# Setup in the MLP's buffers, layer 2's weights decoded beside layer 1, half of the first stores issued by ScalarE: one core of a Trainium2

## The chip, the cores and the metric

One core of one Trainium2 chip runs the whole program. The metric is the device time of one execution in microseconds (us); each kernel is run several times and its median is used. TensorE (PE in the rows) multiplies, VectorE (DVE) and ScalarE (ACT) do element-wise work and empty PSUM, GpSimd (POOL) does element-wise work on SBUF, and SyncE's queue (SP) issues the DMAs. PEld is TensorE's loading of weights.

## The reference

```python
def _attn_ref(x, w_r, w_i, b_r, b_i):          # x: 8 x 3136 x 256
    X = np.fft.rfft(x, axis=1)
    Yr = Xr @ w_r - Xi @ w_i + b_r
    Yi = Xr @ w_i + Xi @ w_r + b_i
    lam = 0.01
    Yr = np.sign(Yr) * np.maximum(np.abs(Yr) - lam, 0.0)
    Yi = np.sign(Yi) * np.maximum(np.abs(Yi) - lam, 0.0)
    y = np.fft.irfft(Y, n=x.shape[1], axis=1)

def _moe_ref(x, U, V, w_ch1, w_ch2):           # U: 3136 x 32, V: 32 x 3136
    xt = x.transpose(0, 2, 1)
    h = xt @ U @ V
    u = x + h.transpose(0, 2, 1)
    ch = np.maximum(u @ w_ch1, 0.0) @ w_ch2    # 256 -> 1024 -> 256
    return u + ch
```

U, V, w_ch1 and w_ch2 arrive as 64-bit floats, and the kernel makes 32-bit numbers of their words itself; this is what "decode" means below.

## The kernel before, in words

**The work.** The Fourier transform over 3136 = 49 x 64 positions is a chain of stages for each of the 8 batches. Stage A multiplies by the 49-point matrix (`a_mm`, PSUM tiles `psa`, 16 units of 98x512 for a batch) and stores the result in DRAM (`gd`, through the tiles `gs`). Stage B reads it back (`t`), multiplies by the 64-point matrix and its twiddles (`fb`, PSUM `psb`). The mix multiplies by the complex weights (PSUM `psy` in batch 0; `psq` and `pst` later), then comes the shrinking (`rl`, `ys`). Stage C goes back over 64 points (`psc`) and stores in DRAM (`zd`, through `zs`). Stage D reads that (`zt`) and multiplies by constants and by U at once (PSUM `psd`, 32 steps a batch); the result lies in SBUF as `xq`, and its product with U is summed in `pa`, turned by two transposes (`psp`) into `pt`. The MLP then goes over 6 windows of 512 positions a batch: `u_prep` adds the product with V (`psv`) to `xq` and splits it into a high and a low part (`oa`, `ob`, `oc`, `od`), layer 1 takes seven products of blocks with the prepared weights `w1t` (PSUM `psx`, `psy`, `psz`), its ReLU gives `rh` and `rl`, layer 2 multiplies by `w2h` and `w2l` (PSUM `pso`), and the sum goes out through `os`. Most products are three matmuls of split operands; A's first units and stages B and D multiply unsplit 32-bit operands.

**What lies beside what.** While the MLP of batch b runs, A of batch b + 2 and B to D of batch b + 1 are put between its chunks. Batch 0 has nothing to lie beside: its stages A to D run alone, with the decoding of the weights between them. Half of A of batch 1 is done early: units 0 to 3 while D of batch 0 waits for its first input, units 4 to 7 behind D (`turn`).

**The decoding.** `load_words` brings 512 (for V 392) 64-bit words a partition, `decode` makes 32-bit numbers of them with two ScalarE and six or seven VectorE instructions on tiles of 128x512 (`dm`, `dlf`, `dq`, `dp`). There are two pieces of V, two of U, four of `w_ch2` (into `w2h`, `w2l`) and four of `w_ch1` (into `wa`), in the order of the list `jobs`; `combine` makes the seven blocks of `w1t` out of the four `wa`.

**What sets the order.** The code records all operations with their tiles, and a list scheduler (`order`, `forward`, `backward`) with a cost for each operation gives each engine one fixed order, which the hardware then follows. Before the change the recording has two phases. Phase 0 is batch 0 up to `turn`, phase 1 is the MLP with all that lies beside it, and `forward` lets no operation of phase 1 stand ahead of one of phase 0 on its engine. The two phases have pools of SBUF tiles of their own, `setup` (named `sp` in the code) and `mp`, which take the same memory one after the other: `mp` is opened when `setup` is closed.

```python
    for phase, p in enumerate((sp, mp)):
        with tc.tile_pool(name=p.name, bufs=p.bufs) as p.real, tc.manual_schedule():
            prog.trace(engines, phase)
```

**Constants of D.** In batch 0 D's right-hand side is one tile `du` (98 x 32 x 130: 98 numbers of the constant and 32 of the product with U). For later batches a `dt` tile takes the constant's part from the input and the other 32 from a copy in DRAM (`dud`), two DMAs for each four steps.

Of the kernel before, what the change touches and what calls it, by code (L numbers as in the profile page):

```python
# [143 lines left out]
class _Op:  # L144
    __slots__ = "n eng name args kw out cost lag start preds succs unit at phase".split()


class _Program:


    def __init__(self):
        self.ops, self.phase = [], 0
# [10 lines left out]
    def record(self, eng, name, args, kw):  # L163
        op = _Op()
        op.n, op.eng, op.name, op.args, op.kw, op.phase = len(self.ops), eng, name, args, kw, self.phase
        op.preds, op.succs = {}, []
        out = kw["out"] if "out" in kw else args[0]
        views = [v for v in list(args) + list(kw.values()) if isinstance(v, _View)]
        op.out = out
        self.cost(op, out, [v for v in views if v is not out])  # L170
        for v in views:
            self.access(op, v, v is out)
        self.ops.append(op)
        return op

    def cost(self, op, out, ins):
        n = out.ids.size // out.shape[0] if isinstance(out, _View) else 1
        sb = not any(v.buf.space == "psum" for v in ins)
        if op.eng == "pe":
# [16 lines left out]
        else:  # L196
            some = out if isinstance(out, _View) else ins[0]

            op.cost, op.lag = max(0.6, some.ids.size / 53760), 2.2
# [32 lines left out]
    def order(self):  # L232
# [24 lines left out]
        def gap(e, op):  # L257

            if e.eng == op.eng and e.eng != "sp":
# [10 lines left out]
        frees = {}  # L270
        for bufs in tags.values():
            k = max(b.bufs for b in bufs)
            for a, b in zip(bufs, bufs[k:]):
                for op in a.users:
                    frees.setdefault(op.n, []).append(b.first[0])

        after, ahead = [{} for _ in units], [{} for _ in units]
        for k, u in enumerate(units):
            for op in u:
                for s in op.succs + frees.get(op.n, []):  # L280
# [3 lines left out]
        for k, d in enumerate(after):  # L284
            for j, g in d.items():
                ahead[j][k] = g
# [11 lines left out]
        for _ in range(PASSES):  # L298
            end, starts = self.forward(units, size, tags, gap, late)
            if best is None or end < best[0]:  # L300
                best = end, starts, self.idle
            late = self.backward(units, size, after, ahead, starts, end)
# [6 lines left out]
    def backward(self, units, size, after, ahead, starts, end):  # L309

        free = {}
# [37 lines left out]
    def forward(self, units, size, tags, gap, late):  # L349
# [3 lines left out]
        left = {(e, p): 0 for e in engines for p in range(self.phase + 2)}  # L353
        wait = [0] * len(units)
        avail = [0.0] * len(units)
        for k, u in enumerate(units):
            left[u[0].eng, u[0].phase] += 1
            for op in u:
                wait[k] += sum(e.unit != k for e in op.preds.values())
        closed = {}  # L360
        for k, u in enumerate(units):
            if u[0].phase and any(left[u[0].eng, p] for p in range(u[0].phase)):
                wait[k] += 1
                closed.setdefault((u[0].eng, u[0].phase), []).append(k)
        slots = {key: [0.0] * max(b.bufs for b in bufs) for key, bufs in tags.items()}
# [17 lines left out]
        def grant(key):  # L383
            bufs = tags[key]
            while turn[key] < len(bufs) and slots[key]:
                b = bufs[turn[key]]
                turn[key] += 1
                t = _heapq.heappop(slots[key])
# [11 lines left out]
        while done < len(units):  # L400
# [20 lines left out]
            for op in units[k]:  # L421
# [8 lines left out]
                for b in bs.values():  # L430
                    b.left -= 1
                    b.end = max(b.end, op.start + op.cost + op.lag)
                    if b.left == 0:
                        _heapq.heappush(slots[b.key], b.end)
                        grant(b.key)
            p = units[k][0].phase
            left[e, p] -= 1
            if left[e, p] == 0:
                for q in range(p + 1, self.phase + 1):
                    if not any(left[e, r] for r in range(q)):  # L440
                        for j in closed.pop((e, q), []):
                            release(j, free[e])
        return max(free.values()), starts

    def trace(self, engines, phase):
# [3 lines left out]
        for op in sorted((o for o in self.ops if o.phase == phase), key=lambda o: (o.start, o.n)):  # L449
# [5 lines left out]
def fft_mix_moe_kernel(  # L455
# [24 lines left out]
    fp, qp, sp, mp = _Pool("fp", 2), _Pool("qp", 2), _Pool("setup", 1), _Pool("mp", 1)  # L480
# [49 lines left out]
    dud = dram.tile([NP, NI, R], F32, name="dud")  # L530
# [37 lines left out]
    def a_mm(b, u):  # L568
# [12 lines left out]
        dma.dma_start(gv[:, 2 * u : 2 * u + 2, :], gs)  # L581
# [29 lines left out]
    def load_fb(b, q):  # L611
# [3 lines left out]
        if b:  # L615
            fbt = fp.tile([128, 2, 128], F32, tag="fb", name=f"fb_{b}_{q}")
        else:
            fbt = first_w["pool"].tile([128, 2, 128], F32, tag="fb0", name=f"fb_{b}_{q}", bufs=5)
# [269 lines left out]
    def d_load(b, t, du):  # L888
        z_load(b, 2 * t)
        z_load(b, 2 * t + 1)  # L890
        if du is None:
            dt_ = mp.tile([NP, TI, NP + R], F32, tag="dt", name=f"dt_{b}_{t}", bufs=2)
            i = slice(TI * t, TI * t + TI)
            dma.dma_start(dt_[:, :, 0:NP], c_fd[:, i, 0:NP])
            dma.dma_start(dt_[:, :, NP:], dud[:, i, :])
        else:
            dt_ = du[:, TI * t : TI * t + TI, :]
# [61 lines left out]
    words = {}  # L959

    def load_words(src, shape, name):
# [7 lines left out]
    def decode(name, hi=None, lo=None, full=None):  # L969
# [43 lines left out]
    first_w["pool"] = sp  # L1013
# [4 lines left out]
    wz = sp.tile([128, 256], F32, name="wz")  # L1018
# [28 lines left out]
    b4r = sp.tile([128, D], F32R, name="b4r")  # L1047
    one = sp.tile([128, 128], F32R, name="one")
# [26 lines left out]
    fcs = sp.tile([128, 192], F32, name="fcs")  # L1075
# [16 lines left out]
    us = sp.tile([NP, NI, R], F32, name="us")  # L1092
    vt = dict(r=sp.tile([128, 64], F32, name="vraw"))
# [6 lines left out]
    du = sp.tile([NP, NI, NP + R], F32, name="du")  # L1100
# [17 lines left out]
    def make_ud(c):  # L1118
        ps = psm([128, 512], f"psu_{c}")
        for k in range(8):  # L1120
            mm = pe.matmul(
# [585 lines left out]
```

## Time and profile before

| | |
|---|---|
| median of 3 runs | 1751.05 us (1749.66 to 1752.8) |
| the profiled execution | 1750.79 us, its span from the first to the last instruction 1749.0 us |
| TensorE busy | 1685.0 us, 96% of the span |
| VectorE busy | 1330.8 us, 76% |
| ScalarE busy | 1029.7 us, 59% |
| GpSimd busy | 579.1 us, 33% |
| DMA queue of SP | 203.38 MB, 45.1% of the 16 DMA engines' span |
| mean granted clock of TensorE | 0.978 of full speed (2.4 GHz) |

The first instruction starts at 0. Stage A of batch 0 runs to about 27 us, B to C from 34 to 101 us, D from 108.8 to 126.3 us. Layer 1 starts at 174.09 us. Matmuls are pipelined, so a row's own duration is longer than its step: 12 matmuls of 128x256 stand in the chain of waits with 1.44 us. The granted clock shows whether TensorE ran at 1.2 (0.5) or 2.4 GHz (1.0).

### The profile page before, as it was taken

What the parts mean: (1) busy time and instruction counts of PE and PEld (TensorE: products, weight loads), DVE (VectorE), ACT (ScalarE), POOL (GpSimd) and SP (SyncE); (2) the same over time, 40 slices, a digit from 0 to 9 for tenths busy, and PEclk for the clock granted to TensorE, in tenths of its full rate; (3) what the DMA queues carried; (4) which work ended last, traced back from release to release, by engine and by line L of the source; (5) the groups of instructions that cost most, each with busy time, mean ns of one, the idle gap of its engine ahead of it and who ended that gap; (6) DMA issues with size and microseconds to landing.
All of it is one profiled execution on the core that took longest, in us unless ns stands there. A gap on an engine that the chain in (4) does not pass through costs nothing.

```text
span 1749.0 us, 31800 instructions
## 1 busy us (share of the span) xinstructions
PE 1685.0 (96%) x11071; PEld 1512.7 (86%) x11071; DVE 1330.8 (76%) x2476; ACT 1029.7 (59%) x2206; POOL 579.1 (33%) x508
## 2 busy tenths in 40 slices
PE   7982999999999999999999999999999999999998
PEld 4971788999898898999988889999989998998997
DVE  2647799788767887699866988689876887757774
ACT  2763677566667665555557665556566565554443
POOL 0211464233434543133343543223344232212221
PEclk8985999999999999999999999999999999999999
DMA  6865465543466543523357543443356432332112
GB/s 214 215 199 138 131 175 147 144 107 84 105 169 179 157 111 91 126 75 87 78 147 202 155 129 78 113 101 88 79 128 184 110 83 37 80 97 51 37 31 37
DMA packets 284690, 205.42 MB, mean 117 GB/s; under 512 B 173506, under 2 KB 237766, under 8 KB 284530
## 3 DMA queue, kind: packets, MB, share of 16 engines
q1 hardware_dynamic: 284530, 203.38, 45.1%
q8 instruction: 89, 1.46, 0.3%
q14 instruction: 71, 0.58, 0.1%
HBM read 124.11 MB, written 79.18 MB: 116 GB/s over the span
## 4 chain that ended last, share of the span: by engine, by line
PE 90%; DVE 5%; DMA 2%; issue 1%; ACT 0%; POOL 0%; SPq 0%; DVEq 0%; POOLq 0%; ACTq 0%
PE pso L451 30%; PE psy L451 17%; PE psx L451 8%; PE psd L451 7%; PE psq L451 7%; PE psb L451 5%; PE psa L451 4%; PE psz L451 4%; PE psc L451 4%; PE pst L451 3%; DVE ys L451 1%; PE psv L451 1%; DVE rl L451 1%; DMA xt<-in_x_dram 1%; DVE tb L451 0%
## 5 line engine op out<-in xcount | busy, mean ns | idle before, releaser
L451 PE MATMUL pso<-rh,w2h 128*128 128x512 f32 x784 | 251.0, 402 | 0.0
L451 PE MATMUL pso<-rl,w2h 128*128 128x512 f32 x784 | 244.1, 393 | 1.0 <-DVE rl L451 1.0
L451 PE MATMUL pso<-rh,w2l 128*128 128x512 f32 x784 | 244.3, 393 | 0.0
L451 POOL TENSOR_TENSOR xl<-xt,xh 98x512 fp32r<-98x512 f32 x104 | 139.4, 1340 | 241.3 <-ACT xh L451 241.0
L451 DVE SCALAR_TENSOR_TENSOR ys<-tb,rl 64x256 f32<-64x256 f32 x350 | 195.2, 558 | 10.6 <-ACT rl L451 5.9
L451 POOL TENSOR_TENSOR yl<-ys,yh 128x512 fp32r<-128x512 f32 (+1 forms) x101 | 133.9, 1326 | 197.4 <-ACT yh L451 194.5
L451 ACT ACTIVATE rh<-s 128x512 fp32r<-128x512 f32 x196 | 123.4, 631 | 97.1 <-DVE s L451 95.6
L451 PEld LDWEIGHTS pso<-rl,w2h 128*128 128x128 f32 x784 | 147.2, 188 | 34.8 <-DVE rl L451 1.8
L451 PEld LDWEIGHTS pso<-rh,w2l 128*128 128x128 f32 x784 | 147.6, 188 | 33.9
L451 DVE SCALAR_TENSOR_TENSOR rl<-s,rh 128x512 fp32r<-128x512 f32 x196 | 159.9, 819 | 9.3 <-ACT rh L451 6.7
L451 POOL TENSOR_TENSOR tl<-ts,th 128x256 fp32r<-128x256 f32 x88 | 70.3, 799 | 235.3 <-ACT th L451 188.8
L451 PEld LDWEIGHTS pso<-rh,w2h 128*128 128x128 f32 x784 | 126.0, 189 | 6.9
L451 PE MATMUL psy<-odh,w1t 128*128 128x256 f32 x784 | 125.5, 282 | 0.7 <-DVE s L451 0.7
L451 PE MATMUL psd<-dt,zt 98*128 98x130 f32 x896 | 124.6, 275 | 0.1
L451 ACT ACTIVATE xq<-psd 128x196 f32<-128x196 f32 x256 | 84.0, 332 | 69.0 <-PE psd L451 60.5
L451 DVE TENSOR_TENSOR v<-v,psy 128x512 f32<-128x512 f32 x98 | 67.0, 684 | 75.4 <-ACT v L451 36.0
L451 PEld LDWEIGHTS psd<-dt,zt 98*128 98x128 f32 x896 | 117.3, 190 | 6.0 <-DVE tt L451 0.3
L451 PEld LDWEIGHTS psy<-odh,w1t 128*128 128x128 f32 x784 | 110.4, 188 | 7.9 <-DVE s L451 1.5
L451 PE MATMUL psb<-fb,t 128*128 128x128 f32 (+1 forms) x800 | 107.0, 277 | 8.4 <-DVE tb L451 6.6
L451 POOL TENSOR_TENSOR ocl<-xq,och 128x256 fp32r<-128x256 f32 x47 | 35.6, 758 | 235.3 <-ACT och L451 235.2
L451 PEld LDWEIGHTS psb<-fb,t 128*128 128x128 f32 (+1 forms) x800 | 100.2, 193 | 13.6 <-DVE tb L451 7.5
L451 ACT ACTIVATE xsh<-psb 128x256 fp32r<-128x256 f32 (+1 forms) x176 | 58.0, 379 | 80.2 <-PE psb L451 80.1
(208 smaller groups left out, 4551.6 us busy)
## 6 DMA issues: line engine op xcount, KB each, us to landing
gd<-gs SPq DMA_DIRECT2D x128, 196.0 KB
zt<-zd SPq DMA_DIRECT2D x128, 196.0 KB
t<-gd SPq DMA_DIRECT2D x192, 128.0 KB
zd<-zs SPq DMA_DIRECT2D x192, 128.0 KB
out_dram<-os SPq DMA_DIRECT2D x192, 128.0 KB
xt<-in_x_dram SPq DMA_DIRECT2D x112, 196.0 KB
fb<-in_fb_dram SPq DMA_DIRECT2D x96, 128.0 KB
vw<-vd SPq DMA_DIRECT2D x96, 128.0 KB
```

Source lines behind the costliest of these rows:

```text
L451: call(*[real(a) for a in op.args], **{k: real(a) for k, a in op.kw.items()})
```

## The change

- **No border.** The pool `setup`, the phases and their gate in `forward` are gone. Every tile of the setup takes a tag of the MLP's pool `mp` (or of `fp`): the loaded words `dw` lie in `rh`, the decoder's tiles in `sv`, U and `wa` in `rl`, `du` as eight tiles of four steps in `oh`, `ol` and `dt`.
- **Layer 2's weights.** The four `w_ch2` pieces leave `jobs`. `w2_unit` decodes them after the setup: piece 0 ahead of window 0, the others as side work at 1, 5 and 9 of window 0's 16 chunks. They are loaded into `ww` (a third slot of `xq`) and `rh`.
- **The order of the rest.** `jobs` is now V, U, the first piece of `w_ch1`, V's second step, the other three pieces, `combine`.
- **Stores of A.** In batch 0 the stores of the even units are issued by ScalarE's queue.
- **Constants of D.** `dud` holds whole rows of 130; eight stores write them from `du`, and a `dt` tile is one DMA of 98x520 numbers.
- **The scheduler** takes a DMA's size as size/67500, at least 0.55, and `backward` follows the slots that `forward` really gave.

```diff
-    fp, qp, sp, mp = _Pool("fp", 2), _Pool("qp", 2), _Pool("setup", 1), _Pool("mp", 1)
+    fp, qp, mp = _Pool("fp", 2), _Pool("qp", 2), _Pool("mp", 1)
...
-        dma.dma_start(gv[:, 2 * u : 2 * u + 2, :], gs)
+        (dma if b or u % 2 else act).dma_start(gv[:, 2 * u : 2 * u + 2, :], gs)
...
-            dma.dma_start(dt_[:, :, 0:NP], c_fd[:, i, 0:NP])
-            dma.dma_start(dt_[:, :, NP:], dud[:, i, :])
+            dma.dma_start(dt_, dud[:, i, :])
...
-        w = first_w["pool"].tile([128, 1024], U32, tag="dw", name="dw_%s%d%d" % name, bufs=3)
+        if name in place:
+            w = place[name]
+        else:
+            w = mp.tile([128, 1024], U32, tag="rh", name="dw_%s%d%d" % name, bufs=3)
...
-    du = sp.tile([NP, NI, NP + R], F32, name="du")
+    du = [
+        mp.tile([NP, TI, NP + R], F32, tag=tg, name=f"du_{t}", bufs=2 if tg == "dt" else 3)
+        for t, tg in enumerate(("oh", "ol", "oh", "ol", "oh", "ol", "dt", "dt"))
+    ]
...
-    jw2 = [(lambda f=f: load_w(2, f), lambda f=f: decode_w2(f)) for f in range(4)]
-    jobs += jw2[:1]
-    jobs += [(load_v4, make_v), (lambda: None, lambda: iter(()))]
-    jobs += jw2[1:]
     jobs += [
         (lambda i=i, h=h: load_w(1, i, h), lambda i=i, h=h: decode_w1(i, h))
         for h in range(2)
         for i in range(2)
     ]
+    jobs[5:5] = [(load_v4, make_v)]
...
-    on(133, lambda: dma.dma_start(dud, du[:, :, NP:]))
+    for t in range(NT):
+        on(116 + 2 * t, lambda t=t: dma.dma_start(dud[:, TI * t : TI * t + TI, :], du[t]))
...
-    prog.phase = 1
...
+    ww = qp.tile([128, 3, 1024], U32, tag="xq", name="ww", bufs=3)
+
+    def w2_unit(n):
+        f = (0, 2, 1, 3)[n]
+        if n < 3:
+            place[2, f, 0] = ww[:, n]
+        load_w(2, f)
+        for _ in decode_w2(f):
+            pass
+
+    w2_unit(0)
...
+                    side += [(at, lambda n=n: w2_unit(n + 1)) for n, at in enumerate((1, 5, 9))]
...
-    for phase, p in enumerate((sp, mp)):
-        with tc.tile_pool(name=p.name, bufs=p.bufs) as p.real, tc.manual_schedule():
-            prog.trace(engines, phase)
+    with tc.manual_schedule():
+        prog.trace(engines)
```

Three places of the fixed orders follow. The first is VectorE from the end of D of batch 0: `pa` is the running sum over D's steps, `pr` and `pt` prepare it for the product with V. Before:

```order
L451 TENSOR_TENSOR pa_1166<-pa_1166,psd_31_1338 128x64
L451 COPY pr_1348<-pa_1166 128x256
L451 TENSOR_SCALAR dm_1353<-dm_1353 128x512
L451 TENSOR_TENSOR pt_1357<-psp_1351,pt_1357 64x256
L451 TENSOR_SCALAR dm_1353<-dm_1353 128x512
L451 SCALAR_TENSOR_TENSOR dq_1368<-dw_1024,dm_1353 128x512
L451 TENSOR_SCALAR dp_210_1371<-dq_1368 128x512
L451 TENSOR_TENSOR dp_210_1371<-dlf_1361,dp_210_1371 128x512
L451 TENSOR_TENSOR dq_1368<-dq_1368,w2h 128x512
L451 TENSOR_TENSOR w2l<-dq_1368,dp_210_1371 128x512
```

Now, from the last instruction of `combine` on:

```order
L442 TENSOR_TENSOR w1t<-s_1277,w1t 128x512
L442 TENSOR_TENSOR pa_1250<-pa_1250,psd_26_1409 128x64
L442 TENSOR_TENSOR pa_1250<-pa_1250,psd_27_1415 128x64
L442 TENSOR_TENSOR pa_1250<-pa_1250,psd_28_1421 128x64
L442 TENSOR_TENSOR pa_1250<-pa_1250,psd_29_1426 128x64
L442 TENSOR_TENSOR pa_1250<-pa_1250,psd_30_1431 128x64
L442 TENSOR_TENSOR pa_1250<-pa_1250,psd_31_1439 128x64
L442 COPY pr_1452<-pa_1250 128x256
L442 TENSOR_SCALAR dm_1454<-dm_1454 128x512 x2
L442 TENSOR_TENSOR pt_1462<-psp_1456,pt_1462 64x256
L442 SCALAR_TENSOR_TENSOR dm_1454<-ww,dm_1454 128x512
L442 TENSOR_TENSOR xq_0_1238<-xq_0_1238,psv_0_1472 128x16x32
```

Before, three pieces of `w_ch2`, four of `w_ch1` and `combine` stood between `pt` and the first sum with `psv`; now all of `w_ch1` stands ahead of D's end, and only three instructions of the first piece of `w_ch2` stand there.

The second place is TensorE from there to the first product of layer 1 (`psy<-obh,w1t`). Before, behind `psd_31`, `psp` and units 4 and 5 of A (`psa`, batch 1):

```order
L451 MATMUL psa_6_1522<-xt_6_1411,fas 98x512
L451 MATMUL psv_0_1537<-vw_1526,pt_1357 128x512
L451 MATMUL psv_1_1539<-vw_1526,pt_1357 128x512
L451 MATMUL psa_7_1557<-xt_7_1461,fas 98x512
L451 MATMUL psa_8_1565<-xh_8_1551,fah 98x512
L451 MATMUL psa_8_1565<-xh_8_1551,fal 98x512
L451 MATMUL psa_8_1565<-xl_8_1555,fah 98x512
L451 MATMUL psr_1575<-vr,pt_1357 128x64 x2
L451 MATMUL psa_9_1589<-xh_9_1571,fah 98x512
L451 MATMUL psa_9_1589<-xh_9_1571,fal 98x512
L451 MATMUL psa_9_1589<-xl_9_1580,fah 98x512
L451 MATMUL psy_0_1599<-obh_1577,w1t 128x256 x4
```

Now:

```order
L442 MATMUL psd_31_1439<-du_1177,zt_15_1391 128x130 x2
L442 MATMUL psa_4_1444<-xt_4_1282,fas 98x512
L442 MATMUL psp_1456<-ident,pr_1452 128x128 x2
L442 MATMUL psv_0_1472<-vw_1240,pt_1462 128x512
L442 MATMUL psv_1_1476<-vw_1240,pt_1462 128x512
L442 MATMUL psa_5_1478<-xt_5_1450,fas 98x512
L442 MATMUL psa_6_1493<-xt_6_1468,fas 98x512
L442 MATMUL psa_7_1502<-xt_7_1474,fas 98x512
L442 MATMUL psy_0_1512<-obh_1491,w1t 128x256 x4
L442 MATMUL psy_0_1512<-obl_1499,w1t 128x256 x2
```

Units 8 and 9 of A and `psr` have moved behind the first products of layer 1.

The third place is SP's queue behind D's last input `zt_15`. Before, some `vd` stores on (`dw` are words to decode, `xt` the inputs of A's units 4 to 8):

```order
L451 DMA dw_1366<-in_moe_w_ch_dram 128x2x512
L451 DMA dw_1373<-in_moe_w_ch_dram 128x2x512
L451 DMA dw_1380<-in_moe_w_ch_dram 128x1024
L451 DMA xt_4_1388<-in_x_dram 98x512
L451 DMA dw_1393<-in_moe_w_ch_dram 128x1024
L451 DMA xt_5_1404<-in_x_dram 98x512
L451 DMA gd_1117<-gs_3_1148 98x512
L451 DMA xt_6_1411<-in_x_dram 98x512
```

Now:

```order
L442 DMA zt_15_1391<-zd_599 98x512
L442 DMA ww<-in_moe_w_ch_dram 128x2x512
L442 DMA dud<-du_852 98x520
L442 DMA gd_1203<-gs_2_1226 98x512
L442 DMA vw_1240<-vd 64x512
L442 DMA xt_5_1450<-in_x_dram 98x512
L442 DMA gd_1203<-gs_3_1311 98x512
L442 DMA dud<-du_863 98x520
L442 DMA xt_6_1468<-in_x_dram 98x512
L442 DMA xt_7_1474<-in_x_dram 98x512
```

Between the first `zt` load and `xt_7` the queue now holds 16 loads of `zt`, four stores of `dud`, three of `gd`, four loads of `xt`, two of `vw` and one of `ww`.

## Rows read from the trace of the kernel before

**Rows 1.** The page, TensorE's busy tenths in 40 equal slices of the span.
```profile
PE   7982999999999999999999999999999999999998
```

**Rows 2.** Stretches: length, busy PE, PEld, DVE, ACT, POOL, clock, DMA share, GB/s.
```profile
0.00:34.10 34.10, 27.59 (x59) 12.08 (x59) 7.78 (x12) 8.43 (x14) 2.36 (x17) 0.90 0.72 224
34.10:108.80 74.70, 72.19 (x524) 65.58 (x525) 40.65 (x64) 50.03 (x102) 17.59 (x14) 0.95 0.77 204
108.80:126.30 17.50, 17.50 (x129) 17.32 (x128) 6.68 (x31) 10.98 (x32) 0.00 (x0) 0.83 0.66 198
126.30:174.10 47.80, 12.29 (x22) 4.99 (x22) 37.45 (x64) 20.41 (x36) 7.44 (x5) 0.52 0.56 145
174.10:325.00 150.90, 145.47 (x942) 128.42 (x941) 136.01 (x226) 104.57 (x223) 77.93 (x66) 0.99 0.52 147
```

**Rows 3.** Timeline from D's end to layer 1: start, duration, engine, instruction.
```profile
127.41 0.41 PE L451 MATMUL psp<-ident,pr 128*128 128x128 f32 x2 [1.10 <-DVE pr L451]
...
128.27 0.43 DVE L451 TENSOR_TENSOR pt<-psp,pt 64x256 fp32r<-64x256 f32 x1 [0.59 <-ACT pt L451]
...
163.10 0.69 DVE L451 TENSOR_TENSOR w1t<-s,w1t 128x512 fp32r<-128x512 f32 x1
...
167.66 1.19 PE L451 MATMUL psv<-vw,pt 128*128 128x512 f32 x2 [24.59 <-DMA xt<-in_x_dram]
...
168.47 1.28 DVE L451 TENSOR_TENSOR xq<-xq,psv 128x512 f32<-128x512 f32 x2 [4.68 <-PE psv L451]
...
172.04 0.62 ACT L451 ACTIVATE obh<-xq 128x512 fp32r<-128x512 f32 x1
...
174.09 1.05 PE L451 MATMUL psy<-obh,w1t 128*128 128x256 f32 x4
```

**Rows 4.** Waits of SP's queue, first 200 us: total, times, longest.
```profile
SPq L451 <- DVE w1t L451: 17.1, 1, 17.1
```

**Rows 5.** Chain of waits: start, length, what; A in three passes and unsplit.
```profile
96.82 1.72 PE psa L451 x4
...
597.55 0.70 PE psa L451 x3
```

**Rows 6.** Timeline, TensorE's second half of stage A and its first B.
```profile
17.59 8.78 PE L451 MATMUL psa<-xx,fas 98*98 98x512 f32 x14 [2.12 <-DMA xx<-in_x_dram]
...
34.15 2.28 PE L451 MATMUL psb<-fb,t 128*128 128x128 f32 x16 [1.77 <-DMA t<-gd]
```

**Rows 7.** VectorE by form, 127 to 164 us: total and mean ns.
```profile
L451 DVE TENSOR_TENSOR dp<-dlf,dp 128x512 f32<-128x512 f32 x7 | 5.7, 819 | 0.7
L451 DVE TENSOR_SCALAR dp<-dq 128x512 uint32<-128x512 uint32 x7 | 4.9, 696 | 0.2
L451 DVE SCALAR_TENSOR_TENSOR dq<-dw,dm 128x512 uint32<-128x512 uint32 x7 | 4.8, 692 | 0.2
...
L451 DVE TENSOR_SCALAR dm<-dm 128x512 f32<-128x512 f32 x7 | 2.9, 421 | 1.1 <-ACT dm L451 1.1
...
L451 DVE TENSOR_TENSOR w2l<-dq,dp 128x512 fp32r<-128x512 f32 x3 | 2.1, 687 | 0.0
```

**Rows 8.** VectorE by form, 167 to 325 us.
```profile
L451 DVE SCALAR_TENSOR_TENSOR wt<-wrs,wis 128x512 f32<-128x512 f32 x1 | 1.8, 1789 | 0.0
```

**Rows 9.** Stretches of 25 us in the MLP's first pass, columns as above.
```profile
275.00:300.00 25.00, 22.69 (x144) 19.44 (x143) 24.47 (x41) 17.68 (x41) 14.34 (x13) 1.00 0.50 144
300.00:325.00 25.00, 25.00 (x165) 22.41 (x164) 23.94 (x41) 14.48 (x29) 9.33 (x9) 1.00 0.47 114
325.00:350.00 25.00, 24.90 (x183) 23.21 (x182) 15.42 (x42) 13.12 (x35) 1.68 (x2) 1.00 0.67 165
```

**Rows 10.** Timeline, VectorE beside GpSimd in the decoding.
```profile
145.53 1.45 POOL L451 TENSOR_TENSOR w1t<-wa,w1t 128x512 fp32r<-128x512 f32 x1 [2.22 <-ACT w1t L451]
145.88 1.37 DVE L451 TENSOR_SCALAR dp<-dq 128x512 uint32<-128x512 uint32 x1
```

More of the change, by code (lines that the diff above doesn't have):

```diff
@@ L144 @@
 class _Op:
-    __slots__ = "n eng name args kw out cost lag start preds succs unit at phase".split()
+    __slots__ = "n eng name args kw out cost lag start preds succs unit at".split()
 class _Program:
     def __init__(self):
-        self.ops, self.phase = [], 0
+        self.ops = []
     def engine(self, eng):
@@ L178, in cost @@
         sb = not any(v.buf.space == "psum" for v in ins)
-        if op.eng == "pe":
+        if op.name == "dma_start":
+            some = out if isinstance(out, _View) else ins[0]
+            op.cost, op.lag = max(0.55, some.ids.size / 67500), 2.2
+        elif op.eng == "pe":
             if op.name == "matmul" and op.kw["lhsT"].buf.dtype == F32:
@@ L269, in order @@
                     v.buf.first = (op,)
[L270 to L277, printed above, removed]
+        after = [{} for _ in units]
         for k, u in enumerate(units):
             for op in u:
-                for s in op.succs + frees.get(op.n, []):
+                for s in op.succs:
                     if s.unit != k:
@@ L298, in order @@
         for _ in range(PASSES):
-            end, starts = self.forward(units, size, tags, gap, late)
+            end, starts, reuse = self.forward(units, size, tags, gap, late)
             if best is None or end < best[0]:
                 best = end, starts, self.idle
-            late = self.backward(units, size, after, ahead, starts, end)
+            late = self.backward(units, size, after, reuse, gap, starts, end)
         end, starts, self.idle = best
@@ L307, in order, with backward @@
         return end
-    def backward(self, units, size, after, ahead, starts, end):
+    def backward(self, units, size, after, reuse, gap, starts, end):
+        after = [dict(d) for d in after]
+        for a, b in reuse:
+            for op in a.users:
+                for j in b.takers:
+                    if j != op.unit:
+                        g = gap(op, b.first[0]) - (b.first[0].at if j == b.first[0].unit else 0)
+                        after[op.unit][j] = max(after[op.unit].get(j, g), g)
+        ahead = [{} for _ in units]
+        for k, d in enumerate(after):
+            for j, g in d.items():
+                ahead[j][k] = g
         free = {}
@@ L356, in forward @@
         for k, u in enumerate(units):
-            left[u[0].eng, u[0].phase] += 1
             for op in u:
                 wait[k] += sum(e.unit != k for e in op.preds.values())
[L360 to L365, printed above, removed]
+        slots = {key: [(0.0, -1, None)] * max(b.bufs for b in bufs) for key, bufs in tags.items()}
+        reuse = []
         turn = dict.fromkeys(tags, 0)
@@ L433, in forward, with trace @@
                     if b.left == 0:
-                        _heapq.heappush(slots[b.key], b.end)
+                        _heapq.heappush(slots[b.key], (b.end, k, b))
                         grant(b.key)
[L436 to L445, printed above, removed]
+        return max(free.values()), starts, reuse
+    def trace(self, engines):
         def real(v):
             return v.get() if isinstance(v, _View) else v
-        for op in sorted((o for o in self.ops if o.phase == phase), key=lambda o: (o.start, o.n)):
+        for op in sorted(self.ops, key=lambda o: (o.start, o.n)):
             call = getattr(engines[op.eng], op.name)
@@ L529, in fft_mix_moe_kernel @@
     zd = [dram.tile([N1, N2, D], F32, name=f"zd{k}") for k in range(2)]
-    dud = dram.tile([NP, NI, R], F32, name="dud")
+    dud = dram.tile([NP, NI, NP + R], F32, name="dud")
     vd = dram.tile([2, R, 96 * NI], F32, name="vd")
@@ L959, in fft_mix_moe_kernel @@
     words = {}
+    place = {}
     def load_words(src, shape, name):
@@ L1137, in decode_v @@
     def decode_v(c):
-        full = sp.tile([128, 392], F32, tag="dfull", name=f"full_{c}")
+        full = mp.tile([128, 392], F32, tag="tt", name=f"full_{c}")
         yield from decode(("v", c, 0), full=full)
@@ L1158, in make_v @@
             vh, vl = [
-                sp.tile([128, 512], F32R, tag=tg, name=f"{tg}v{k}", bufs=2)[0:96] for tg in ("d1", "d2")
+                mp.tile([128, 512], F32R, tag="sv", name=f"v{tg}{k}", bufs=4)[0:96] for tg in "hl"
             ]
```

75 lines of the change are left out of this document (38 added, 37 removed).

## The prediction

> **What bounds the kernel now.** I read the page's slices first. TensorE is busy for nine tenths or more of 36 of the 40 slices; the fourth, from 131 to 175 us, shows 2 tenths [rows 1]. So the kernel is bound by TensorE except at its start and there. The stretches give that hole its size: between D's last matmul (126.3) and layer 1's first (174.1) lie 47.8 us, in which TensorE is busy for 12.3, at a granted clock of 0.52, which is the lower of its two levels, 1.2 GHz; VectorE is busy for 37.5 [rows 2]. The timeline says what ends the hole. The transposes `psp` are done at 127.8 and `pt` at 128.7. VectorE then decodes and combines weights until 163.8. The loads `vw`, which belong to the MLP's pool, come only after that, so `psv` starts at 167.66, and `psy` at 174.09 [rows 3]. The trace puts `psv`'s wait of 24.6 us down to an input of A; SP's own waits show the cause, 17.1 us in one wait for the last `w1t` of VectorE [rows 3, 4]. That is the border: one tile of the old pool still in use holds the queue, and every load of the MLP stands behind it.
>
> Behind 174 us there is little to gain: in the next 150.9 us TensorE is idle for 5.4, VectorE for 14.9 [rows 2]. Ahead of 126 us, B to C is busy for 72.2 of 74.7 us; stage A for 27.6 of 34.1 [rows 2], partly at the lower clock.
>
> **The change part by part.** The sum is made against the profiled execution's span of 1749.0 us; its time was 1750.79, so 1.8 us lie around the span, and the median of the runs, 1751.05, is 0.3 above it.
>
> *The border and the decoding of `w_ch1`: -39.3 us.* In the new order the last `w1t` of VectorE stands ahead of D's step 26, so from D's end to layer 1 only a chain is left: `psp` and `pt`, 2.4 us (126.3 to 128.7); from `psv`'s start to the end of the two sums on `xq` 2.1 us (167.66 to 169.75); `obh` 0.62, and a tenth to start `psy` [rows 3]. That is 5.2 us, the lower bound. But three units of A stand ahead of `psy` on TensorE, in order, and `psa_7` needs `xt_7`. By the order SP issues, from the first `zt` on, 16 `zt`, 4 `xt` and 3 `gd` (98x512 numbers of 4 bytes, 0.2 MB), 4 `dud` (98x520, 0.2 MB), 2 `vw` (0.13 MB) and `ww` (0.52 MB): 6.2 MB, of which 6.0 come after the first `zt`. In D the DMAs now move 198 GB/s with the engines 0.66 busy, in B 204 at 0.77 [rows 2], so 265 to 300 if they never paused; I take 240. The first `zt` is there at 108.8 [rows 2], so `xt_7` lands at 108.8 + 25 = 133.9; one unit of A (0.86, [rows 5]) later `psy` starts, at 134.8. The gap left is 8.5 us, and 47.8 - 8.5 = 39.3. At today's 198 GB/s it would be 13.8 (upper bound). D itself keeps its 17.5 us: up to `zt_15` the queue holds 4.2 MB, 17.3 us at 240 GB/s. ScalarE has two instructions on `ww` ahead of `pt`'s copy, and VectorE three; `ww` is issued right behind `zt_15`, and if it is late, `pt`, `psv` and layer 1 wait behind them in order. That is inside the two bounds.
>
> *Work moved behind `psy`: +1.6 us.* Units 8 and 9 of A at 0.70 each [rows 5] and `psr` (0.2) filled the hole; now they stand between layer 1's products, where TensorE is full.
>
> *`w_ch2` beside layer 1: +4.0 us.* A piece takes seven VectorE instructions: twice 0.421 on `dm`, 0.692, 0.696, 0.819, and twice 0.687, together 4.4 us, 17.7 for four [rows 7]. Three of them (1.5) lie ahead of the first sum, and `wt` (1.8, [rows 8]) leaves this stretch for the early setup, so VectorE gets 14.4 us more. It had 14.9 idle in 150.9 [rows 2], so the cover is just used up. The fullest 25 us had VectorE at 24.5, 98%, and TensorE lost 2.3 there; the next 25, with 23.9, lost nothing [rows 9]. Filled to 98% the stretch needs (136.0 + 14.4) / 0.98 = 153.5 us, 2.6 more; and TensorE's loss at such fullness, the mean of those two, is 1.15 in 25 us or 6.9 in the stretch, 1.5 more than now. Together 4. The lower bound is 0, since behind 325 us VectorE idles 9.6 of 25 [rows 9] and the work beside layer 1 can slide there; the upper one is the first rival. ScalarE's 12 instructions for this lie in the 46 us that it idles here.
>
> *Stage A: -2.0 us.* Half the stores leave SP's queue, and ten loads of x now stand ahead of its first store. TensorE's second half of A is held by the loads: 7 units take 8.8 us at the lower clock, 1.25 each against 0.86 [rows 5, 6]. What moves until B's start at 34.15 is 224 GB/s for 34.1 us, 7.6 MB [rows 2, 6]; at 240 GB/s it takes 31.8. Bounds: 0 and -5 (at 265 GB/s). ScalarE now waits for VectorE's copies and for the stores it issues, behind which its own copies queue; it idles 26 of 34 us here [rows 2].
>
> *Setup in B to C: +1.0 us.* The four `w_ch1` pieces (six instructions each, 3.73 us) and `combine` (eight of 0.69) now run beside B and D, and one `w_ch2` piece (4.4) leaves [rows 7]: 14.9 + 5.5 - 4.4 = 16 us more on VectorE, which idles 34 of 74.7 us in B to C and 10.8 of 17.5 in D [rows 2]. The cover is large, but queues are in order: `ys` of a unit can stand behind a decode step. Bounds: 0, and 1 us for each of B's 13 units, 13.
>
> *Nothing:* 56 DMA issues fewer for `dt`, the scheduler's new costs elsewhere. From 350 us on TensorE is busy in nearly every slice [rows 1], and the number of matmuls is unchanged.
>
> Sum: -39.3 + 1.6 + 4.0 - 2.0 + 1.0 = -34.7; the span is 1714.3 us, the time **1716 us**, 2.0% faster.
>
> **The rivals.**
>
> *Decoding collides with GpSimd.* A VectorE instruction of a kind that takes 0.42 took 1.37 us where it fell into a GpSimd instruction of 1.45 [rows 7, 10]. Beside layer 1 GpSimd is busy in 78 of 150.9 us [rows 2], against 7.4 of 47.8 in the hole where the prices above come from. If each of the 25 remaining instructions meets one with that chance, they cost 25 x 0.52 x 0.95 = 12.3 us more, with no idle time left to take them: 1728 us. Against it: the slack behind 325 us [rows 9], and a hit may cost less than the whole instruction. The Trainium skill ("SBUF — State Buffer", section "Who interferes with whom") has a rule for this: VectorE and GpSimd share a port pair, and whichever takes it first keeps the other out for its whole instruction. The row of 1.37 us agrees; by the rule every such meeting is paid in full, and the time would be this rival's 1728. Chance 0.16.
>
> *Another wait takes the border's place.* `oh`, `ol` and `dt` are now freed by D's steps and by the `dud` stores; `od`'s tile waits for the fifth store, which stands behind `xt_8`. With the DMAs at 198 GB/s and TensorE kept at 1.2 GHz behind the lull, layer 1 begins 5 us later and its first 15 us of work run at half rate, 7 us lost: 1728 to 1732. For it speaks the clock of 0.52 in the hole [rows 2]. Chance 0.08. That the border stays whole can't be: the orders show `w1t` ahead of D's end.
>
> *All cover holds.* Gap 5.2, `w_ch2` free, A at its bound: 1716 - 3.3 - 4 - 3 = 1706. Chance 0.08.
>
> *Slower: the setup's chain holds B back.* The decode steps wait for their loads in the middle of VectorE's and ScalarE's queues, and `ys`, `yh` and the split of `psb` wait behind them, in each of B's 13 units. A unit takes 72.2 / 13 = 5.6 us of TensorE. At 4 us of waiting a unit the time is 1716 + 51 = 1767; from 2.8 us on the change is slower. Against it: VectorE is busy in only half of B to C [rows 2], and loads stand far ahead of their use. Chance 0.03.
>
> **How the numbers follow.** The forecast's own case, 1708 to 1724, has 0.64; the rivals have 0.16, 0.08, 0.08 and 0.03, and 0.01 is left for no change. 1703 to 1734 reaches over the first three rivals and the bounds of the gap (-3.3, +5.3) and of stage A, and leaves out a B that loses much more than a us a unit. This kernel's runs spread by about 0.2%, so that is the least that can be told from no change: faster 0.95, same 0.01, slower 0.04.
>
> **What would show it.** The stretch from D's last `psd` to the first `psy` should be 6 to 12 us long, with no wait of SP for `w1t`. If `psa_7` waits for an input, the DMAs set it. In the 150 us behind, VectorE should be busy at 95% or more and TensorE lose 8 to 12 us; more than 20 would be the first rival, with `dp` at well over 0.8 us. B's first matmul should start near 32 us, and B to D should take as long as now within 3 us. The prediction is wrong if VectorE's queue shows long waits for `dw` in B, or if the hole is above 15 us.

## The result, and the profile after

The changed kernel takes **1730.0 us** (median of 4 runs, 1728.67 to 1732.31) where the kernel before took 1751.9 in the same session (1749.66 to 1756.13): 0.9874 of the time, 95% interval 0.9850 to 0.9897. That is 1.26% faster, inside the predicted range and on the predicted side, but 22 us gained where 35 were forecast. The profiled execution took 1732.31 us, its span 1730.5, against the 1749.0 of the sum: 18.5 us.

The page's slices for the changed kernel, as in [rows 1], and the new queue of ScalarE:

```profile
PE   8989999999999999999999999999999999999998
...
q10 hardware_dynamic: 896, 1.61, 0.3%
```

The hole in the fourth slice is gone. The stretches, cut at the same events as [rows 2] (B's start, D's start, D's end, layer 1's start, and 150.9 us behind it):

```profile
0.00:34.10 34.10, 26.07 (x59) 11.33 (x59) 10.54 (x18) 11.20 (x20) 5.95 (x20) 0.95 0.75 242
34.10:111.60 77.50, 72.85 (x525) 65.95 (x526) 47.80 (x78) 52.33 (x110) 19.60 (x15) 0.95 0.79 220
111.60:127.30 15.70, 15.70 (x130) 15.44 (x129) 11.42 (x38) 12.21 (x38) 1.40 (x1) 0.94 0.91 286
127.30:134.40 7.10, 5.63 (x11) 1.95 (x10) 5.57 (x13) 4.89 (x10) 0.00 (x0) 0.76 0.68 229
134.40:285.30 150.90, 143.05 (x899) 124.11 (x898) 140.37 (x229) 102.20 (x219) 72.04 (x60) 0.98 0.55 157
```

The gap between D and layer 1 is 7.1 us long, where it was 47.8. B's start hasn't moved. In the 150.9 us behind layer 1's start TensorE is busy 2.4 us less than before and has done 43 matmuls fewer. The timeline of the gap, answering to [rows 3] (start, duration, instruction):

```profile
125.73 0.69 DVE L442 TENSOR_TENSOR w1t<-s,w1t 128x512 fp32r<-128x512 f32 x1
...
128.65 0.41 PE L442 MATMUL psp<-ident,pr 128*128 128x128 f32 x2 [0.53 <-DVE pr L442]
...
129.99 0.79 PE L442 MATMUL psv<-vw,pt 128*128 128x512 f32 x2 [0.94 <-DVE pt L442]
130.58 4.42 PE L442 MATMUL psa<-xt,fas 98*98 98x512 f32 x6
...
133.06 0.62 ACT L442 ACTIVATE obh<-xq 128x512 fp32r<-128x512 f32 x1
...
134.43 1.04 PE L442 MATMUL psy<-obh,w1t 128*128 128x256 f32 x4
```

The last `w1t` of VectorE now ends at 126.4, ahead of D's end. Between `psv` and `psy` stand three units of A, and they wait for no input. They run at a granted clock of 0.5 (from 130.5 to 134.0 us) and take 3.85 us; `obh`, which `psy` needs, is ready at 133.7, so they hold layer 1 back for the last 0.7 us.

**Where the time went.** I gave each of the 11,071 matmul records its kind's usual distance to the next one, and asked when each kernel had done the same amount. Times are those of the kernel before: a lead of 40 us at 180 means that the changed kernel had done at 140 us what the other had done at 180. The changed one is 0.9 us behind at 125 us, **40.2 ahead at 180, 31.4 at 300**, 28.6 at 980, 21.4 at 1500 and 18.9 at 1720. So it loses 8.8 us in the first 120 us of layer 1, and then 12.5 more, in many places, where I had forecast nothing.

### The profile page after: what moved, and what is told of

It is laid out like the page before. It is cut to its first block, busy times and chain, and to the rows that moved or that the text cites. A ratio compares the mean times of both kernels' runs of the same rounds, so it can differ in the third digit from the quotient of the medians.

```text
span 1730.5 us, 31661 instructions
## 1 busy us (share of the span) xinstructions
PE 1692.2 (98%) x11071; PEld 1516.8 (88%) x11071; DVE 1355.2 (78%) x2476; ACT 1032.1 (60%) x2210; POOL 578.5 (33%) x508
## 3 DMA queue, kind: packets, MB, share of 16 engines
q8 instruction: 88, 1.44, 0.3%
## 4 chain that ended last, share of the span: by engine, by line
PE 83%; DVE 9%; DMA 3%; issue 2%; ACT 1%; SPq 1%; POOL 0%; DVEq 0%; ACTq 0%; POOLq 0%
PE pso L442 29%; PE psy L442 15%; PE psx L442 7%; PE psd L442 7%; PE psq L442 6%; PE psb L442 4%; PE psa L442 4%; PE psz L442 4%; PE psc L442 3%; PE pst L442 3%; DVE ys L442 2%; DVE rl L442 1%; PE psv L442 1%; DVE tb L442 1%; DMA gd<-gs 1%
## 5 line engine op out<-in xcount | busy, mean ns | idle before, releaser
L442 DVE SCALAR_TENSOR_TENSOR ys<-tb,rl 64x256 f32<-64x256 f32 x350 | 208.9, 597 | 8.7 <-ACT rl L442 4.0
L442 DVE SCALAR_TENSOR_TENSOR rl<-s,rh 128x512 fp32r<-128x512 f32 x196 | 172.5, 890 | 10.0 <-ACT rh L442 7.7
L442 PEld LDWEIGHTS pso<-rl,w2h 128*128 128x128 f32 x784 | 147.0, 188 | 34.3 <-DVE rl L442 1.2
L442 PEld LDWEIGHTS pso<-rh,w2h 128*128 128x128 f32 x784 | 130.4, 189 | 13.0
L442 PE MATMUL psy<-odh,w1t 128*128 128x256 f32 x784 | 129.3, 287 | 1.0 <-DVE v L442 0.7
L442 DVE TENSOR_TENSOR pa<-pa,psd 128x64 f32<-128x64 f32 x248 | 53.8, 217 | 73.5 <-ACT xq L442 68.4
L442 POOL TENSOR_TENSOR ocl<-xq,och 128x256 fp32r<-128x256 f32 x47 | 39.3, 837 | 209.9 <-ACT och L442 198.6
```

The source lines that it names most:

```text
L442: call(*[real(a) for a in op.args], **{k: real(a) for k, a in op.kw.items()})
```

## The experiments

Twelve kernels ran, each 4 to 6 times, beside the kernel before on the same chip. "Ahead" and "behind" are by the count of equal work above.

**1. Layer 2's weights copied, not decoded** (`w2_copied`).

```diff
-        for _ in decode_w2(f):
-            pass
+        v = words.pop((2, f, 0))
+        for k, o in enumerate(w2s):
+            acopy(o[:, 2 * f : 2 * f + 2].rearrange("p f d -> p (f d)"), f32(v[:, :, 1 - k]))
```

> The changed kernel, but w_ch2's words are only copied into w2h and w2l by two ScalarE instructions a piece where they were decoded (the decoding of w_ch2 is left out); loads and places stay. Set against the kernel before on equal work, the changed kernel led by 40 us when layer 1 began, by 31 us some 90 us later and by 18.5 at the end. Theory A (decoding beside layer 1 fills VectorE): the 9 us lost in the 90 us after layer 1's start go down to 2 or less, VectorE is busy for less than 90% there, time 1720 to 1723. Rival B (layer 1's start itself: one window's operands, units of A in between, TensorE at 1.2 GHz): the same 7 to 9 us are lost, time 1728 to 1731.

Measured: 1728.7 us, 0.9877 (0.9863 to 0.9892). The stretch behind layer 1's start:

```profile
137.80:288.70 150.90, 145.47 (x943) 130.13 (x942) 127.65 (x217) 106.08 (x229) 72.71 (x63) 0.99 0.58 166
```

VectorE is busy 12.7 us less than in the changed kernel, TensorE 2.4 more with 44 matmuls more, and the lead stands still: 35.5 us at 180, 36.1 at 300. So theory A holds for this stretch: without the decoding those 8.8 us aren't lost. Not all of them are waits for VectorE. In the changed kernel TensorE also falls to the lower clock, after 11.3 us in which it was busy for 8.7:

```profile
150.00:161.30 11.30, 8.73 (x44) 6.14 (x43) 11.06 (x15) 7.90 (x16) 7.09 (x6) 1.00 0.78 210
161.30:168.10 6.80, 6.00 (x20) 5.09 (x21) 6.01 (x9) 5.04 (x10) 3.47 (x3) 0.50 0.46 145
```

In `w2_copied` TensorE stays at the upper clock from 147.0 to 1720 us. The total time is theory B's all the same. It hardly fell because this kernel's order starts B at 39.46 us, 5 later; that was no part of the edit's purpose, and I had left such shifts out of the expectation. With a changed list of operations the scheduler gives the whole kernel a new order, so the edit isn't the only difference.

**2. The four pieces in the setup's list again** (`w2_in_setup`): `jobs` as before the change, `w2_unit` gone.

> The changed kernel with w_ch2's four pieces decoded in the setup's list again, in the places of the kernel before (no border). Theory A: the 17.7 us of VectorE work fit under B, C and D, where VectorE idles 34 us now; the loss after layer 1's start goes to 3 us, the gap ahead of it stays at 8 to 12 us; time 1721 to 1727. Rival B: no loss is saved after layer 1's start, and the four pieces push the last w1t behind D's end: gap 20 us or more, time 1738 or more.

Measured: 1733.6 us, 0.9908 (0.9891 to 0.9924). The gap is 10.5 us, and the lead goes from its highest, 36.7 us at 200, to 32.9 at 300: the work fits under B to D, as theory A says, and only 4 us are lost behind layer 1's start, with TensorE once more at the lower clock (205.7 to 209.1 us). The time is above theory A's; B again starts late (38.66 us), which takes 3 us.

**3. The scheduler as it was** (`old_planner`).

```diff
-            op.cost, op.lag = max(0.55, some.ids.size / 67500), 2.2
+            op.cost, op.lag = max(0.6, some.ids.size / 53760), 2.2
...
-        for a, b in reuse:
...
+                for s in op.succs + frees.get(op.n, []):
```

> The changed kernel with the scheduler's cost of a DMA and its backward pass as they were. Theory A: the 12 us that the changed kernel loses from 300 us on, a little in every batch, come of the new order; they go down to 4 or less: time 1718 to 1724. Rival B (the loss there is of the whole rows for D, or of the later slots that the border's end gives): it stays, time 1728 to 1732.

Measured: 1785.7 us, **1.0195** (1.0171 to 1.0218). Both theories are wrong: with the old scheduler the change makes the kernel 34 us slower. VectorE's longest wait between 120 and 240 us (total, times, longest):

```profile
DVE oal L442 <- DMA dud<-du: 14.4, 1, 14.4
```

The timeline of this run where layer 1 begins:

```profile
221.61 0.78 PE L442 MATMUL psx<-oah,w1t 128*128 128x256 f32 x2
...
222.25 0.68 DVE L442 TENSOR_TENSOR w1t<-wa,w1t 128x512 fp32r<-128x512 f32 x1
```

And 25 us around it, columns as in [rows 2]:

```profile
200.00:225.00 25.00, 16.30 (x72) 13.34 (x73) 22.92 (x36) 14.65 (x32) 10.88 (x9) 0.70 0.64 193
```

With no border to hold them, the old scheduler puts decode steps of `w_ch1` behind D, among batch 1's stages, where they are still at work at 222 us; an operand of layer 1 waits 14.4 us for a slot that a store of `du` still reads, until 159.3 us; and layer 1 starts at 221.6 us. TensorE has batch 1's units to do meanwhile, but a lead of some 32 us at 180 turns into 24.7 behind at 300. The wait for a slot is what my second rival named; decode steps of `w_ch1` that still run at 222 us are in none of my rivals.

**4. All stores of A on SP** (`sp_stores`): `dma.dma_start(gv[...], gs)`.

> The changed kernel with all stores of A issued by SP again. Theory A (the DMAs and the late loads of t bound the start, not the queue that issues): B's first matmul at 34 to 35 us as now, time 1729 to 1732. Rival B (ScalarE's queue saves time that something else ate): B starts at 36 to 39 us, time 1732 to 1735.

Measured: 1734.9 us, 0.9915 (0.9899 to 0.9930); B starts at 35.97 us; theory B is the nearer one. So the second queue is worth some 2 us at the start, and 2 (by the spans) to 7 us (by the ratios) in all. The Trainium skill ("DMA: Bandwidth & Descriptors", section "Issuing engines are not separate DMA queues") says that another issuing engine saves only the time to issue. The 1.8 us at B's start agree with that as a small gain.

**5. The old cost of a DMA alone** (`old_dma_cost`): the first line of experiment 3's diff.

> The changed kernel with the scheduler's old cost of a DMA but the new backward pass; with both old it took 1785.7 us, since layer 1's operand oal waited 14.4 us for a store of du and layer 1 went on late. Theory A (the backward pass, which follows the slots that were really given, is what gets du's stores and w_ch2 in time): 1728 to 1736. Rival B (the smaller cost of a DMA does): 1770 or more.

Measured: 1745.8 us, 0.9966 (0.9954 to 0.9978), between the two: of the 56 us that the new scheduler is worth in the changed kernel, 40 come with the backward pass, and 16 more with the cost. Neither theory gave this time, and the new cost without the new backward pass wasn't run.

**6. The new scheduler in the kernel before** (`before_new_planner`): both parts of experiment 3's diff the other way round, nothing else; the border stands.

> The kernel before with the scheduler's new cost of a DMA and its new backward pass, nothing else. Theory A (the new order costs TensorE 5 to 9 us of waits from 300 us on, whatever the start does): the border's gap stays at 46 to 50 us, time 1755 to 1761. Rival B (the new scheduler is better everywhere, and what is lost from 300 us on comes of the rest of the change): 1735 to 1750.

Measured: **1739.0 us, 0.9926** (0.9911 to 0.9940), rival B. The stretches of B to C, D and the gap:

```profile
34.10:110.50 76.40, 71.47 (x523) 66.95 (x524) 59.25 (x94) 57.06 (x115) 18.19 (x14) 0.92 0.85 229
110.50:130.30 19.80, 18.85 (x132) 17.25 (x131) 14.14 (x46) 13.14 (x37) 1.93 (x2) 0.88 0.94 263
130.30:144.60 14.30, 6.97 (x20) 3.27 (x19) 8.99 (x16) 6.63 (x15) 2.72 (x2) 0.81 0.62 149
```

SP's wait that answers to [rows 4]:

```profile
SPq L453 <- DVE w1t L453: 4.2, 1, 4.2
```

And the timeline of the end of the gap:

```profile
136.85 0.68 DVE L453 TENSOR_TENSOR w1t<-s,w1t 128x512 fp32r<-128x512 f32 x1
137.73 1.17 SPq L453 DMA_DIRECT2D vw<-vd  x2
...
141.45 1.19 PE L453 MATMUL psv<-vw,pt 128*128 128x512 f32 x2 [7.06 <-DMA vw<-vd]
...
144.56 1.06 PE L453 MATMUL psy<-obh,w1t 128*128 128x256 f32 x4
```

The first row begins 1.9 us ahead of B, which starts at 36.03 us here; D's last matmul ends at 130.46, so the gap is 14.1 us. VectorE is busy for 58 us in B to C where it was 41 [rows 2]: the new scheduler decodes there, all four pieces of `w_ch2` too. The border now holds SP's queue for 4.2 us instead of 17.1. So 33.7 of the gap's 47.8 us can be had by the order alone; the rest of the change, the border's end among it, gives the last 7.

**7. Slots 32 bytes wider in the kernel before** (`before_wide_slots`). From 300 us on, two things differ between the kernels. One is more short waits (below). The other is smaller than any wait: in the last 150 us, where only layers 1 and 2 are left, a matmul of layer 1 of 256 columns follows the one before it after 113 ns in the kernel before, 118 in the changed one. `du` had widened the slots of `oh` and `ol` from 2048 to 2080 bytes, and the experiment does only that:

```diff
+    for k in "hl":
+        pad = mp.tile([128, 520], F32, tag=f"o{k}", name=f"pad{k}", bufs=3)
+        pool.memset(pad[:, 0:1], 0.0)
```

> The kernel before, in which the slots of oh and ol are 2080 bytes wide instead of 2048 (as in the changed kernel, where du lies in them), by two small GpSimd memsets; the order of TensorE, VectorE, ScalarE and the DMAs is the same. In the last 120 us of layer 1 alone, a 256-column matmul follows the one before it after 113 ns in the kernel before and after 118 ns in the changed one. Theory A (where the operands lie in SBUF sets this pace): 117 to 119 ns there now, 4 to 7 us lost over the whole run, time 1755 to 1759. Rival B (order, queues or DMAs set the pace): 113 to 114 ns, time 1750 to 1753.

Measured: 1760.2 us, **1.0048** (1.0035 to 1.0062), 8.4 us slower in the same order, a little more than theory A allowed. TensorE's timeline in the kernel before:

```profile
1650.93 0.62 PE L451 MATMUL psy<-odh,w1t 128*128 128x256 f32 x4
1651.38 0.39 PE L451 MATMUL psy<-odl,w1t 128*128 128x256 f32 x2
...
1652.97 0.62 PE L451 MATMUL pso<-rh,w2h 128*128 128x512 f32 x2
```

And in this one:

```profile
1651.10 0.64 PE L451 MATMUL psz<-obh,w1t 128*128 128x256 f32 x4
1651.57 0.40 PE L451 MATMUL psz<-obl,w1t 128*128 128x256 f32 x2
...
1652.52 0.63 PE L451 MATMUL pso<-rh,w2h 128*128 128x512 f32 x2
```

The 18 matmuls from 1650.93 to 1652.97 are 113 ns apart, the 12 from 1651.10 to 1652.52 are 118. Over the last 120 us the mean is 113.9 in the kernel before, 118.8 here and 118.0 in the changed kernel. Theory A holds: where the operands lie sets the pace.

**8. Slots of 2112 bytes in the changed kernel** (`after_2112_slots`): `du`'s tiles in `oh` and `ol` get 528 numbers a row.

> The changed kernel with slots of oh and ol of 2112 bytes, so that all of them begin at the same offset within 64 bytes, as in the kernel before. Same order. Theory A1 (the offset within 64 bytes sets the pace): 113 to 114 ns in the last 120 us, time 1724 to 1727. Theory A2 (placement counts, but not by this offset) and rival B: 117 to 119 ns, time 1729 to 1732.

Measured: 1732.6 us, 0.9891 (0.9877 to 0.9905), 118.3 ns, as theory A2 has it. The offset within 64 bytes is not it.

**9. The MLP's tiles moved by 64 bytes, in the kernel of experiment 6** (`before_planner_shift`). The new order also lays tiles out anew, and experiment 6 shows 119.8 ns: its operands of layer 1 begin at 416 bytes modulo 512, like the weights (all but one, `ocl`, at 480). In the kernel before they begin at 480.

```diff
+            if phase:
+                p.real.tile([128, 16], F32, name="pad", tag="pad", bufs=1)
```

`dt`'s slots are 2304 bytes wide besides, so that what lies behind them moves alike.

> The kernel before with the new scheduler (1739.0 us, 119.7 ns from one 256-column matmul of layer 1 to the next in the last 120 us), its MLP tiles moved by 64 bytes and dt's slots widened to 2304, so that all operands of layers 1 and 2 begin at 480 bytes modulo 512 and their weights at 416, as in the kernel before; there the operands of layer 1 stood at 416, like the weights. Same order. Theory A (the offset of moving operand to weights sets the pace): 113 to 114 ns in the last 120 us, time 1731 to 1734. Rival B (something else of the layout or the order): 118 to 120 ns, time 1737 to 1741.

Measured: **1726.3 us, 0.9865** (0.9846 to 0.9883), 12.7 us better than experiment 6, in the same order (7.1 by the profiled spans). The time is below both theories. The pace is 116.6 ns in the last 120 us, between them: 113 in some windows, 118 in others, though the operands lie as in the kernel before.

**10 and 11. Equal slots in the changed kernel, without and with the 64 bytes** (`after_du_in_os`, `after_du_in_os_shift`): `du` in nine tiles, seven steps of D in `os`, so that `oh` and `ol` have 2048 bytes again; the second one also fetches `w1t` and `w2s` ahead of `wm` and adds the pad of experiment 9.

> The changed kernel with du cut in nine tiles (seven steps of D in os, three in each slot of oh and ol, seven in dt), so that the slots of oh and ol are 2048 bytes again; all operands of the MLP then begin at 416 bytes modulo 512, w1t at 416, w2h and w2l at 160. Theory A (offset): the operands of layer 1 stand like their weights, 119 to 120 ns in the last 120 us; time 1728 to 1733. Rival B (equal slots are enough): 113 to 114 ns, time 1721 to 1726.

> The run above with the MLP's tiles moved by 64 bytes (480 modulo 512) and w1t, w2h, w2l laid out ahead of the other constants (416). Same order. Theory A (offset): 113 to 114 ns in the last 120 us, 5 to 8 us less than the run above, 1721 to 1727. Rival B (offset doesn't matter): the same pace and time as the run above within 2 us.

Measured: 1742.9 us, 0.9962 (0.9949 to 0.9976), at 119.3 ns; and 1734.9 us, 0.9911 (0.9895 to 0.9926), at 114.6 ns. TensorE's timeline without the 64 bytes:

```profile
1629.90 0.64 PE L442 MATMUL psy<-obh,w1t 128*128 128x256 f32 x4
...
1631.34 0.63 PE L442 MATMUL pso<-rh,w2h 128*128 128x512 f32 x2
```

And with them:

```profile
1692.04 0.62 PE L442 MATMUL psz<-obh,w1t 128*128 128x256 f32 x4
...
1693.40 0.62 PE L442 MATMUL pso<-rh,w2h 128*128 128x512 f32 x2
```

12 matmuls take 1.44 us (120 ns) in the one, 1.36 (113 ns) in the other. Same order, 8 us: the place of the operands again; that of layer 2's weights has changed here too (160 to 416). Both lie above the changed kernel; B starts 4 us later in them (38.3 and 38.8 us).

**12. Nearly all of TensorE's operands at that offset** (`before_planner_aligned`): experiment 6 with the tiles of each tag fetched in a chosen sequence before the program is written out, and one pad of 64 bytes.

```diff
...
+    for v in (vr, lam, w1t, *w2s, *fc, *fa, fc0[0], *wm[0], *wm[1], *wm[2], bias, fas, nm):
+        v.get()
+    for tg in ("t", "xt", "xsh", "xsl", "th", "tl"):
+        firsts["fp", tg].get()
+    fp.real.tile([128, 16], F32, name="pad", tag="pad", bufs=1)
+    for tg in ("xh", "xl", "yh", "yl", "fb"):
+        firsts["fp", tg].get()
...
```

> The kernel before with the new scheduler in the same order as the run that took 1739.0 us, but with nearly all operands laid out for TensorE: what is streamed through it (operands of layers 1 and 2, wm, xh, xl, yh, yl, fb, vw) begins at 480 bytes modulo 512, and what is loaded as weights (w1t, w2h, w2l, fch, fcl, fah, xsh, xsl, th, tl, t) at 416; only fal, zt, pt and half of dt don't fit. Theory A (TensorE runs at 113 ns for 256 columns as long as all that it reads one after the other keeps this offset): 113 to 114 ns in most stretches from 300 us on, not only in the last; time 1712 to 1720, below both kernels. Rival B (the stretches with stages A to D beside layer 1 are slower for another reason): 117 to 118 ns there, time 1724 to 1731, as with the shift of the MLP's tiles alone (1726.3).

Measured: **1724.1 us, 0.9857** (0.9839 to 0.9875), the fastest median of all; its interval overlaps the changed kernel's. The pace from 300 us on is 116.8 ns on average against 119.5 in experiment 6, with whole windows of 20 us at 113.3 and others at 118. So each theory is right in some windows, and the time is rival B's. Why is open.

## Why the prediction was right, and where it was mis-sized

The direction and the range were right, and the range in part by luck. 1730 us is outside my own case (1708 to 1724); it is near where the first two rivals would have put it, and neither came as I described it. What filled the difference is a loss that I had at nothing. Of the signs that I named, the gap and the length of B to D came true; B's first matmul started at 34.1 us and not near 32, VectorE was busy at 93% and not 95% beside layer 1, and TensorE lost 7.9 us there where I had said 8 to 12.

**The border and the decoding of `w_ch1`, -39.3: right in size, half right in cause.** The gap was to be 8.5 us and is 7.1; `psa_7` found its input there. D, which I had kept at 17.5 us, took 15.7. That is the clock: D's matmuls follow each other after 217 ns at the lower level and 112 at the upper one in both kernels, and the lower one lasted for the first 6.1 us of D before and for 2.1 now. The DMAs moved 286 GB/s in D, more than the 240 I took. But I read the 17.1 us wait of SP as the price of the border. Experiments 3 and 6 show that the order decides: with the border and the new scheduler 33.7 us are gained; without the border and with the old scheduler nothing is, and layer 1 starts 47.5 us later than before the change.

**"Nothing": the scheduler's new costs elsewhere.** This is the step that failed, with one that the sum didn't have: where the operands lie, now that `du` has widened the slots of `oh` and `ol`. The scheduler is worth 12.8 us in the kernel before and 55.6 in the changed one. And from 300 us on, where I had seen a full TensorE and an equal number of matmuls, 12.5 us are lost. Set against each kind's shortest distance in the trace before, the distances hold 4.7 us more in pieces below 30 ns (the pace of experiment 7) and 8.9 more in longer ones, with some 50 more of 80 ns or above. The profile shows little of that as waiting: TensorE's idle time on this work is 7.7 us against 5.4. The longest waits from 300 to 1700 us (total, times, longest), the kernel before first:

```profile
PE psb L451 <- DVE tb L451: 5.2, 2, 2.6
...
PE psa L442 <- DVE tb L442: 2.5, 2, 1.4
PE psq L442 <- DVE xsl L442: 2.2, 4, 0.7
PE psc L442 <- DVE tb L442: 1.0, 2, 0.6
```

Experiment 6 has 4.7 of the 8.9 us, so about half of it comes with the new order alone; the cause of the rest stays open.

**`w_ch2` beside layer 1, +4.0: measured 8.8** (experiment 1). VectorE is busy at 93% of the 150.9 us, less than the 95% that I named, and still TensorE lost more than I allowed. My mean over the stretch hid that the load is uneven: from 150 to 161 us VectorE is busy at 98% and TensorE at 77% (rows in experiment 1). On the same work TensorE's idle time grew by 3.5 us (7.9 against 4.4). The 6.8 us at half the clock behind 161 us cost some 3 more (an estimate: layer 1's matmuls follow each other after 213 ns there, for 118 at the upper clock); I had no term for that. The first rival is in it at under a third of its price. Forms of the decode from 129 to 300 us, answering to [rows 7]:

```profile
L442 DVE TENSOR_TENSOR dp<-dm,dp 128x512 f32<-128x512 f32 x4 | 5.1, 1274 | 0.2
...
L442 DVE TENSOR_SCALAR dp<-dm 128x512 uint32<-128x512 uint32 x4 | 3.8, 939 | 0.0
L442 DVE TENSOR_TENSOR w2l<-dm,dp 128x512 fp32r<-128x512 f32 x4 | 3.5, 870 | 0.1
```

These take 455, 243 and 183 ns more each than in the gap, 3.5 us for twelve, where the rival had 12.3. In the timeline six of the twelve are 0.5 to 1.1 us longer than their shortest; each began while a GpSimd instruction was running, and ended 0.3 to 0.6 us after that one:

```profile
150.12 1.46 POOL L442 TENSOR_TENSOR xl<-xt,xh 98x512 fp32r<-98x512 f32 x1 [2.70 <-ACT xh L442]
...
150.54 1.59 DVE L442 TENSOR_TENSOR dp<-dm,dp 128x512 f32<-128x512 f32 x1
```

Two others, during which a GpSimd instruction began, aren't longer. That agrees with the Trainium skill's rule ("SBUF — State Buffer", section "Who interferes with whom") that the first to take the shared ports keeps the other out. The rival's size was wrong: a meeting cost about what was left of the GpSimd instruction and not the whole of it, and seven of the 25 instructions paid, where the rival had 13 (25 x 0.52).

**Stage A, -2.0: measured 0.** TensorE's part of A ended earlier, but B starts where it did:

```profile
34.14 4.71 PE L442 MATMUL psb<-fb,t 128*128 128x128 f32 x24 [3.55 <-DMA t<-gd]
```

The chain of waits has the store ahead of it (start, length, what):

```profile
26.12 4.25 DMA gd<-gs
```

The store lands at 30.4 us, and `t` is read back only then, 3.7 us before B; that more bandwidth shortens this little is argued, not shown. The queue's part alone may have come as forecast: with all stores on SP, B starts 1.8 us later (experiment 4), so something else in the change takes as much away; what, stays open.

**Setup in B to C, +1.0: measured +0.9** at D's end, by luck: 2.8 us more in B to C, of which D gives 1.8 back by its clock. **Moved work, +1.6**, is inside the lead of 40.2 us at 180.

In sum: up to layer 1 the forecast was a lead of 38.7 us, and 40.2 came; `w_ch2` 4.8 more than forecast; from 300 us on 12.5 lost that I had at nothing.

## What to carry to other kernels

When a change comes with new numbers for a list scheduler, price these first and alone: here they alone gave 12.8 of the 22 us, and without them the rest of the change was a loss. A wait named by the trace shows what stands last, not what would stand there under another order. When pools or tags change, compare TensorE's distance from matmul to matmul in a stretch with nothing beside it, before looking for waits: 32 bytes a slot cost 8 us.

## What the runs showed of the hardware

**The place of operands.** A 256-column matmul follows the last one after 113 ns, or after 118 to 120, at the same granted clock of 1.00 and in the same order, by where its operands lie in SBUF. Equal offsets (modulo 512 bytes) of the streamed operand and the weights gave 119 to 120 in layer 1 (experiments 6, 10); mixed offsets 118. The streamed operand 64 bytes above the weights gave 113 to 115 over the last 120 us in the kernel before and in experiment 11, but 116.6 in experiment 9, and in experiment 12 windows of 113 and of 118 alternate. In the kernel before it is 113 for long only with nothing beside layers 1 and 2. So the offset is not all of it, and what else sets the pace is open. The Trainium skill ("SBUF — State Buffer", section "Who interferes with whom") gives TensorE separate read ports for the streamed operand and for the weights and names contention only between VectorE and GpSimd; by that, the place would cost nothing. The measurement decides: at 118 to 120 ns for 113, it costs 4 to 6% of these matmuls' time.

**The clock.** A stage that TensorE fills from end to end can change its length by the clock alone: D took 17.5 us with its first 6.1 us at 1.2 GHz, and 15.7 with 2.1.
